# A seven-product second layer: sums in quarters, another product order, other places for loads and stores

## The chip, the cores and the metric

The kernel runs on one core of a Trainium2 chip. The time is the device time of one execution in microseconds (us); the kernel before takes 1622.39 us (median of 3 runs, 1622.34 to 1624.89). The profiled execution took 1622.71 us, of which 1620.9 us lie between its first and its last instruction (the span). Engines are named as in the profile: PE multiplies matrices, PEld loads its weights, DVE is the vector engine, ACT the scalar engine, POOL the GpSimd engine, SP issues the DMAs.

## The reference

```
q, k, v: (8, 8, 576, 64) f32
for each chunk of 64 tokens of each head:          # attention inside the chunk
    a = softmax(q_c @ k_c.T / sqrt(64)) @ v_c
x = a as (4608 tokens, 512)
x = silu(x @ w_in) @ w_out                         # 512 -> 2048 -> 512
h = x @ w_in2                                      # second network
out = (h * sigmoid(1.702 * h)) @ w_out2            # 4608 x 512
```

The weights come as f64 and are brought to f32 on the chip.

## The kernel before, in words

Every f32 operand is split in two fp32r tiles: a high part (a cast, on ACT) and the rest (operand minus high part, on DVE). A product is three matmuls: high by low, low by high, high by high.

**First stage, up to about 860 us.** Blocks of 512 tokens go through attention and the first network. PE works in steps of 24 matmuls (12 for `h`, 12 for the output). Beside it, every 7 steps, one piece of the second network's weights is prepared (`load_u`, `pack_w`, `combine_u` on POOL, `split_u`): 16 conversions in all. `split_u` runs twice per conversion, first for the four combinations that POOL made (`split_u(..., True)`), then for the three plain quarters. Each call takes one tile from the two-tile pool `r`, casts into it (ACT, L212), subtracts (DVE, L214) and stores it to HBM (L222). On the same DVE queue stand the two transposes `qkT` (L282) of each 128 tokens of attention; the scores on PE (L292) wait for them.

**Second network's first layer, to about 1211 us.** `in_products`, in seven products per 2 by 2 blocks (Strassen's scheme in Winograd's form) instead of eight.

**Second network's second layer, 1211 to 1575 us, where most of the change lies.** `out_products` takes 4 units of 1024 tokens. A unit has four quadrants A11, A12, A21, A22 of the activations (`g` in HBM, 256 KB per 128x512 block) and seven products with prepared weights: A11, A12, A22 and the sums S1 = A21 + A22, S2 = S1 - A11, S3 = A11 - A21, S4 = A12 - S2. Each product runs in 4 steps (`PAIRS`), so a unit has 28 steps, numbered from 0 in it. A step is 12 matmuls of 128x512 into two PSUM banks. The list `SEQ` gives the order of the products.

In a unit, per step: ACT casts an operand of 128x1024 (`high_d`, L938), DVE makes the low part (`low_d`, L943), both three steps ahead of PE. The tile for it comes from the pool `x` with 4 tiles, so the cast of step s+3 waits until PE has finished step s-1. POOL makes the 16 sums of a unit (`sum_d`, L925), 128x1024 each, in place: S1 and S2 and S4 over the tile `mix` (loaded with A21), S3 over the tile `a`. SP loads the other quadrants by `stream` into the pool `g` (3 tiles): a load waits until the third tile before it has been read. After a product's fourth step `finish_d` brings its two banks to SBUF: by two ACT copies (L981) or by two DVE additions to an earlier copy (L985). `turn_d` transposes on DVE (L1018), `store_d` stores (4 DMAs per 128x512).

Each engine works off its own queue in the order in which the program is written: the loop over steps calls, per step, stores, transposes, the entries of a table (`at_d(step, function, ...)`), `high_d` and `low_d` for three steps ahead, then the matmuls, then `finish_d`. The numbers in the table set the places; nothing is timed, an instruction waits only for its data and for the instruction before it.

**The last 512 tokens, 1575 us to the end.** `out_product`, with POOL sums of 128x256 (`sum_r`, L797) and DVE low parts (`split_r`, L810).

The lines that set this are few:

```python
SEQ = (A11, S1, S2, A12, S3, S4, A22)
BANK = {A11: "a", S2: "a", S3: "a", A22: "a", S1: "c", S4: "c", A12: "b"}
x_p = ctx.enter_context(tc.tile_pool(name="x", bufs=4))
g_p = ctx.enter_context(tc.tile_pool(name="g", bufs=LAG + 1))
nc.gpsimd.tensor_tensor(out=out_, in0=one, in1=two, op=op)      # L925
at(after, 0, s + 5, split_u, *key, True)
at(after, 0, s + 7, split_u, *key, False)
```

Of the kernel before, what the change touches and what calls it, by code (L numbers as in the profile page):

```python
# [17 lines left out]
P = 128  # L18
# [31 lines left out]
def chunk_attention_two_ffn(  # L50
# [823 lines left out]
    SEQ = (A11, S1, S2, A12, S3, S4, A22)  # L874
# [39 lines left out]
    def sum_d(u, o, pp):  # L914
# [32 lines left out]
    OPENS = {A11: "a", S1: "c", A12: "b"}  # L947
    BANK = {A11: "a", S2: "a", S3: "a", A22: "a", S1: "c", S4: "c", A12: "b"}

    def open_banks(u, name):  # L950

        if name == "a" and u % 2:
            whole = ps_at.tile([P, 2, N], F32, tag="at", name="ps_m")
            bank_u[u, name] = [whole[:, i] for i in range(2)]
        elif name == "b":
# [4 lines left out]
    def step_d(u, s):  # L960

        o, pp = SEQ[s // PAIRS], s % PAIRS
        if pp == 0 and o in OPENS:
            open_banks(u, OPENS[o])
# [27 lines left out]
    def finish_d(u, o):  # L992

        banks = bank_u[u, BANK[o]]
        if o == A11:
            kept_u["m1"] = [copy_d(st_p, "st", x) for x in banks]
        elif o == S1:
            kept_u["m5"] = [copy_d(v_p, "v", x) for x in banks]
        elif o == S2:
            kept_u["u2"] = [copy_d(*h, x) for h, x in zip(((v_p, "v"), (st_p, "st")), banks)]  # L1000
        elif o == A12:
            done_d.append((u, 0, 0, [add_d(x, y) for x, y in zip(banks, kept_u.pop("m1"))]))
        elif o == S3:
            done_d.append((u, 1, 1, [add_d(x, y) for x, y in zip(banks, kept_u.pop("m5"))]))
        elif o == S4:
            done_d.append((u, 0, 1, [add_d(x, y) for x, y in zip(banks, kept_u.pop("u2"))]))
        else:
            done_d.append((u, 1, 0, [copy_d(st_p, "st", x) for x in banks]))
# [3 lines left out]
    def turn_d():  # L1012

        while done_d:
            u, t, e, parts = done_d.pop(0)
            for i, s in enumerate(parts):
                to = st_p.tile([P, N], F32, tag="st", name="turned")
                nc.vector.transpose(out=to, in_=s)  # L1018
                turned_d.append(((2 * u + t) * N, (2 * e + i) * P, to))

    def store_d():

        while turned_d:
# [13 lines left out]
    def out_products():  # L1037
# [8 lines left out]
        at_d(1, sum_d, 0, S1, 3)  # L1046
# [421 lines left out]
```

## Time and profile before

| | us |
|---|---|
| median of 3 runs | 1622.39 |
| profiled execution | 1622.71 |
| its span | 1620.9 |
| PE busy (97% of the span) | 1564.9 |
| DVE busy (59%) | 959.8 |
| POOL busy (22%) | 352.1 |
| PE idle before matmuls of L970, ended by DVE | 33.3 |

Busy times are averages over stages with different limits. PE counts as busy while a matmul is in flight, so a step whose start was late can still look nearly full; how far apart the steps start says more.

### The profile page before, as it was taken

What the parts mean: (1) busy time and instruction counts of PE and PEld (TensorE: products, weight loads), DVE (VectorE), ACT (ScalarE), POOL (GpSimd) and SP (SyncE); (2) the same over time, 40 slices, a digit from 0 to 9 for tenths busy, and PEclk for the clock granted to TensorE, in tenths of its full rate; (3) what the DMA queues carried; (4) which work ended last, traced back from release to release, by engine and by line L of the source; (5) the groups of instructions that cost most, each with busy time, mean ns of one, the idle gap of its engine ahead of it and who ended that gap; (6) DMA issues with size and microseconds to landing.
All of it is one profiled execution on the core that took longest, in us unless ns stands there. A gap on an engine that the chain in (4) does not pass through costs nothing.

```text
span 1620.9 us, 24335 instructions
## 1 busy us (share of the span) xinstructions
PE 1564.9 (97%) x9226; PEld 1288.5 (79%) x9226; DVE 959.8 (59%) x1445; ACT 729.2 (45%) x1046; POOL 352.1 (22%) x211
## 2 busy tenths in 40 slices
PE   8999999999999999999999999999998999898998
PEld 6778888878887888788888888889876766676788
DVE  6986666666766676566223242424337697786875
ACT  6774444444444444444234454546443343333432
POOL 1000000000000000010110111113018275473935
PEclk9999999999999999999999999999999999999999
DMA  8763454444535444452555424334498554728363
GB/s 243 213 145 77 111 137 124 104 111 111 144 85 137 111 124 105 111 135 80 178 201 183 159 105 167 118 132 163 163 342 318 165 161 130 222 83 241 116 156 79
DMA packets 352951, 242.82 MB, mean 150 GB/s; under 512 B 261696, under 2 KB 284224, under 8 KB 348224
## 3 DMA queue, kind: packets, MB, share of 16 engines
q1 hardware_dynamic: 352832, 241.25, 50.2%
q8 instruction: 72, 1.18, 0.3%
q14 instruction: 47, 0.39, 0.1%
HBM read 155.19 MB, written 85.98 MB: 149 GB/s over the span
## 4 chain that ended last, share of the span: by engine, by line
PE 64%; DVE 10%; DMA 8%; POOL 7%; issue 4%; SPq 4%; ACT 3%; DVEq 0%; POOLq 0%; ACTq 0%
PE h L424 18%; PE acc L459 18%; PE acc L577 17%; DMA rows_s<-g 4%; DVE op L943 3%; POOL mix L925 3%; PE h L577 3%; POOL a L925 2%; PE ps_at L292 2%; PE ps_m L970 1%; SPq L1026 1%; DVE aT L383 1%; PE acc L829 1%; POOL raw_u L199 1%; SPq L257 1%
## 5 line engine op out<-in xcount | busy, mean ns | idle before, releaser
L424 PE MATMUL h<-x,w 128*128 128x512 f32 x1728 | 419.9, 392 | 0.6 <-DVE w L155 0.6
L459 PE MATMUL acc<-g,w 128*128 128x512 f32 x1728 | 416.5, 390 | 1.4 <-DVE w L155 1.2
L459 PEld LDWEIGHTS acc<-g,w 128*128 128x128 f32 x1728 | 323.6, 188 | 69.5 <-DVE w L155 1.9
L424 PEld LDWEIGHTS h<-x,w 128*128 128x128 f32 x1728 | 321.7, 188 | 69.7 <-DVE w L155 1.3
L577 PE MATMUL acc<-operand,t 128*128 128x512 f32 (+1 forms) x1200 | 274.4, 385 | 0.0
L577 PEld LDWEIGHTS acc<-operand,t 128*128 128x128 f32 x1200 | 222.4, 188 | 44.6
L447 DVE TENSOR_TENSOR g<-s,g 128x512 fp32r<-128x512 f32 x144 | 100.1, 697 | 217.5 <-ACT g L437 216.1
L435 ACT ACTIVATE s<-h 128x512 f32<-128x512 f32 x144 | 86.1, 598 | 301.3 <-PE h L424 295.2
L199 POOL TENSOR_TENSOR raw_u<-raw_u 128x256 f32<-128x256 f32 x64 | 52.6, 842 | 693.2 <-DVE raw_u L139 541.1
L970 PE MATMUL acc<-op,t 128*128 128x512 f32 x768 | 180.4, 394 | 8.7 <-DVE op L943 7.7
L970 PEld LDWEIGHTS acc<-op,t 128*128 128x128 f32 x768 | 144.3, 189 | 43.5 <-DVE op L943 12.2
L595 DVE TENSOR_TENSOR s<-acc,u 128x512 f32<-128x512 f32 (+1 forms) x80 | 51.0, 637 | 163.3 <-PE acc L577 120.2
L383 DVE STREAM_TRANSPOSE aT<-e 32x128 f32<-32x128 f32 x448 | 135.5, 303 | 6.0
L943 DVE TENSOR_TENSOR op<-mix,op 128x1024 fp32r<-128x1024 f32 x48 | 110.9, 2345 | 10.2 <-ACT op L938 9.8
L943 DVE TENSOR_TENSOR op<-rows_s,op 128x1024 fp32r<-128x1024 f32 x32 | 63.1, 1977 | 70.1 <-ACT op L938 69.7
L970 PE MATMUL ps_m<-op,t 128*128 128x512 f32 x384 | 94.1, 400 | 9.2 <-DVE op L943 9.2
L590 ACT COPY u<-acc 128x512 f32<-128x512 f32 (+1 forms) x80 | 43.5, 544 | 128.7 <-PE acc L577 128.4
L970 PEld LDWEIGHTS ps_m<-op,t 128*128 128x128 f32 x384 | 72.0, 191 | 30.7 <-DVE op L943 15.9
L925 POOL TENSOR_TENSOR mix<-mix,rows_s 128x1024 f32<-128x1024 f32 x16 | 50.5, 3176 | 201.9 <-DMA rows_s<-g 111.5
L437 ACT CAST g<-s 128x512 fp32r<-128x512 f32 x144 | 89.5, 622 | 4.6
L603 ACT ACTIVATE s<-s 128x512 f32<-128x512 f32 (+1 forms) x120 | 70.8, 591 | 33.8 <-DVE s L595 31.9
L938 ACT CAST op<-rows_s 128x1024 fp32r<-128x1024 f32 x32 | 33.6, 1049 | 116.1 <-DMA rows_s<-g 99.9
(128 smaller groups left out, 1739.7 us busy)
## 6 DMA issues: line engine op xcount, KB each, us to landing
g<-s SPq DMA_DIRECT2D x128, 256.0 KB, 2.1
rows_s<-g SPq DMA_DIRECT2D x128, 256.0 KB, 3.8
t<-w SPq DMA_DIRECT2D x28, 1024.0 KB, 5.4
w<-split_u SPq DMA_DIRECT2D x16, 1024.0 KB, 4.4
w<-split_u SPq DMA_DIRECT2D x16, 768.0 KB, 4.4
x<-o SPq DMA_DIRECT2D x36, 256.0 KB, 2.3
raw<-in_q_dram SPq DMA_DIRECT2D x256, 32.0 KB, 2.2
raw<-in_k_dram SPq DMA_DIRECT2D x256, 32.0 KB, 2.4
```

Source lines behind the costliest of these rows:

```text
L199: nc.gpsimd.tensor_tensor(out=high[:, t - T1], in0=one, in1=two, op=ALU.subtract)
L383: nc.vector.transpose(out=aT_t[t0][to:to + 32, j, u], in_=e[of:of + 32, c, r])
L424: nc.tensor.matmul(out=h[:, :n], lhsT=w[:, 0, a, c * P:(c + 1) * P], rhs=x[b][:, c, :n], start=(c == 0 and (a, b) == TERMS[0]), stop=(c == ...
L435: nc.scalar.activation(out=s[:, :n], in_=h[:, :n], func=ACTF.Silu)
L437: nc.scalar.copy(out=g[:, 0, :n], in_=s[:, :n])
L447: nc.vector.tensor_tensor(out=g[:, 1, :n], in0=s[:, :n], in1=g[:, 0, :n].bitcast(F32), op=ALU.subtract)
L459: nc.tensor.matmul(out=a[:, :n], lhsT=w[:, 1, wi, i * P:(i + 1) * P], rhs=g[:, gi, :n], start=first and (wi, gi) == TERMS[0], stop=last an ...
L577: nc.tensor.matmul(out=bank[:, :n], lhsT=of_t(0, j, WITH[o], a)[:, c * P:(c + 1) * P], rhs=x[:, b, c], start=start and (c, a, b) == terms[ ...
L603: nc.scalar.activation(out=s[:, :n], in_=src[:, :n], func=ACTF.Silu, scale=act_scale[1])
L925: nc.gpsimd.tensor_tensor(out=out_, in0=one, in1=two, op=op)
L943: nc.vector.tensor_tensor(out=t[:, 1], in0=source_d(u, o, pp), in1=t[:, 0].bitcast(F32), op=ALU.subtract)
L970: nc.tensor.matmul(out=bank, lhsT=of_t(1, 2 * pp + c, WITH[o], e)[:, i * P:(i + 1) * P], rhs=x[:, a, c], start=begins, stop=pp == PAIRS - ...
```

## The change

The numbers below are steps of a unit.

1. POOL's sums: one 128x1024 instruction becomes four of 128x256.
2. The products of a unit come as A11 S1 A22 S2 S3 A12 S4 instead of A11 S1 S2 A12 S3 S4 A22. A22 goes to the bank pair "b" and is copied from there (`m4`), and its output is S3's bank plus that copy, a second pair of DVE additions one step after the first (`late`). Bank pair "a" is now always the same two banks.
3. The places in the table: sums S1 at -3, -2, -1, 0, S2 at 2, 4, 5, 7, S3 at 9, 10, 12, 13, S4 at 15, 16, 18, 19 (before: -3 to 0, 2 to 5, 6 to 9, 10 to 13); loads of A22 for its own product at 1, 2, 3, 6 (before 19 to 22), A21 at 7, 8, 9, 11 (before 4 to 7), A12 at 12, 14, 15, 18 (before 8 to 11).
4. Per step one transpose and one store instead of all that are due; stores stand behind the table's entries; `finish_d` runs one step later, behind the `high_d` and `low_d` of that step.
5. First stage: `split_u(..., True)` at s + 6 instead of s + 5.

```diff
-    SEQ = (A11, S1, S2, A12, S3, S4, A22)
+    SEQ = (A11, S1, A22, S2, S3, A12, S4)
...
-            out_, one, two, op = mix, rows_s.pop((u, "a12", pp)), mix, ALU.subtract
-        nc.gpsimd.tensor_tensor(out=out_, in0=one, in1=two, op=op)
+            out_, one, two, op = mix, rows_s[u, "a12", pp], mix, ALU.subtract
+        for c in range(2):
+            for h in (slice(0, N // 2), slice(N // 2, N)):
+                nc.gpsimd.tensor_tensor(
+                    out=out_[:, c, h], in0=one[:, c, h], in1=two[:, c, h], op=op
+                )
...
-    OPENS = {A11: "a", S1: "c", A12: "b"}
-    BANK = {A11: "a", S2: "a", S3: "a", A22: "a", S1: "c", S4: "c", A12: "b"}
+    BANK = {A11: "a", S2: "a", S3: "a", A22: "b", A12: "b", S1: "c", S4: "c"}
+    OPENS = (A11, S1, A22, A12)
...
+        elif o == A22:
+            kept_u["m4"] = [copy_d(st_p, "st", x) for x in banks]
         elif o == S2:
             kept_u["u2"] = [copy_d(*h, x) for h, x in zip(((v_p, "v"), (st_p, "st")), banks)]
+        elif o == S3:
+            done(1, 1, "m5")
+            return lambda: done(1, 0, "m4")
...
-        while done_d:
-            u, t, e, parts = done_d.pop(0)
-            for i, s in enumerate(parts):
...
+        if done_d:
+            t0, d0, s = done_d.pop(0)
...
-                at_d(g + 4 + pp, stream, u, "a21", pp)
-                at_d(g + 8 + pp, stream, u, "a12", pp)
-                at_d(g + 19 + pp, lambda u, pp: stream(u, "a22o", pp), u, pp)
-                at_d(g + 2 + pp, sum_d, u, S2, pp)
-                at_d(g + 6 + pp, sum_d, u, S3, pp)
-                at_d(g + 10 + pp, sum_d, u, S4, pp)
...
+            at_each(u, "a22o", (1, 2, 3, 6))
+            at_each(u, "a21", (7, 8, 9, 11))
+            at_each(u, "a12", (12, 14, 15, 18))
...
+            sums_at(u, S2, (2, 4, 5, 7))
+            sums_at(u, S3, (9, 10, 12, 13))
+            sums_at(u, S4, (15, 16, 18, 19))
...
         for g in range(1, STEPS * NU):
             u, s = divmod(g, STEPS)
-            store_d()
-            turn_d()
             for fn, args in todo.get(g, ()):
                 fn(*args)
...
                 high_d(u3, o3, s3 % PAIRS)
                 low_d(u3, o3, s3 % PAIRS)
...
+            store_d()
+            if late is not None:
+                late()
+                late = None
+            if s % PAIRS == 0:
+                late = finish_d((g - 1) // STEPS, SEQ[(g - 1) % STEPS // PAIRS])
+            turn_d()
             step_d(u, s)
-            if s % PAIRS == PAIRS - 1:
-                finish_d(u, SEQ[s // PAIRS])
...
-            at(after, 0, s + 5, split_u, *key, True)
+            at(after, 0, s + 6, split_u, *key, True)
```

ACT's queue of the first unit around product S2, before (L938 casts an operand, L981 copies a bank). The casts from `mix` are the last two of S2's operands, those from `rows_s` A12's, that from `a11` the first of S3's; the copies from acc1 and acc3 empty S1's banks, those from acc0 and acc2 S2's:

```order
L938 CAST op_11326<-mix_11119 128x1024
L981 ACTIVATE o_11341<-acc1_11266 128x512
L981 ACTIVATE o_11343<-acc3_11267 128x512
L938 CAST op_11349<-mix_11119 128x1024
L938 CAST op_11370<-rows_s_11345 128x1024
L938 CAST op_11389<-rows_s_11366 128x1024
L938 CAST op_11408<-rows_s_11386 128x1024
L981 ACTIVATE o_11423<-acc0_11164 128x512
L981 ACTIVATE o_11425<-acc2_11165 128x512
L938 CAST op_11428<-rows_s_11405 128x1024
L938 CAST op_11446<-a11_10808 128x1024
```

The same queue in the changed kernel (the same two lines are L942 and L982 there), from S2's last cast over A22's copies out of `h` to the first casts of A12; acc0 and acc2 are again S2's banks:

```order
L942 CAST op_11458<-mix_11125 128x1024
L982 ACTIVATE o_11461<-h_11376 128x512
L982 ACTIVATE o_11463<-h_11377 128x512
L942 CAST op_11481<-a11_10808 128x1024
L942 CAST op_11499<-a11_10808 128x1024
L942 CAST op_11521<-a11_10879 128x1024
L942 CAST op_11540<-a11_10879 128x1024
L982 ACTIVATE o_11543<-acc0_11170 128x512
L982 ACTIVATE o_11545<-acc2_11171 128x512
L942 CAST op_11564<-rows_s_11451 128x1024
L942 CAST op_11591<-rows_s_11496 128x1024
```

S2's two copies now stand behind all four casts of the product that follows on PE (S3, from `a11`), the last of which is that of S3's fourth step; and S3 writes the same two banks.

POOL's queue, S2 and S3 of the last unit, before:

```order
L925 TENSOR_TENSOR mix_12212<-mix_12212,rows_s_12305 128x1024
L925 TENSOR_TENSOR mix_12163<-mix_12163,a11_12099 128x1024 x2
L925 TENSOR_TENSOR mix_12212<-mix_12212,a11_12134 128x1024 x2
L925 TENSOR_TENSOR a11_12099<-a11_12099,rows_s_12424 128x1024
L925 TENSOR_TENSOR a11_12099<-a11_12099,rows_s_12445 128x1024
```

and in the changed kernel:

```order
L927 TENSOR_TENSOR mix_12380<-mix_12380,rows_s_12410 128x256 x4
L927 TENSOR_TENSOR mix_12331<-mix_12331,a11_12191 128x256 x8
L927 TENSOR_TENSOR mix_12380<-mix_12380,a11_12214 128x256 x8
L927 TENSOR_TENSOR a11_12191<-a11_12191,rows_s_12610 128x256 x4
L927 TENSOR_TENSOR a11_12191<-a11_12191,rows_s_12632 128x256 x4
```

The sums follow each other as before; only their number of instructions has changed, four for one.

DVE's queue in the first stage, at two of the 16 conversions, as a difference. First the kind whose attention transposes (L282) came right behind the first low part (L214):

```order
 L447 TENSOR_TENSOR g_1891<-s_1889,g_1891 128x512
-L214 TENSOR_TENSOR split_u_1906<-raw_u_1644,split_u_1906 128x4x256
-L282 STREAM_TRANSPOSE qkT_1910<-raw0_1727 128x512
-L282 STREAM_TRANSPOSE qkT_1912<-raw1_1813 128x512
-L447 TENSOR_TENSOR g_1929<-s_1927,g_1929 128x512
+L282 STREAM_TRANSPOSE qkT_1906<-raw0_1727 128x512
+L282 STREAM_TRANSPOSE qkT_1908<-raw1_1813 128x512
+L447 TENSOR_TENSOR g_1925<-s_1923,g_1925 128x512
+L214 TENSOR_TENSOR split_u_1949<-raw_u_1644,split_u_1949 128x4x256
```

The transposes now stand ahead of the low part. Then the kind whose transposes come behind the second low part; they follow after the last row shown:

```order
-L214 TENSOR_TENSOR split_u_2710<-raw_u_2390,split_u_2710 128x4x256
-L383 STREAM_TRANSPOSE aT_2714<-e_2660 32x128 x16
-L447 TENSOR_TENSOR g_2746<-s_2744,g_2746 128x512
+L383 STREAM_TRANSPOSE aT_2710<-e_2660 32x128 x16
+L447 TENSOR_TENSOR g_2742<-s_2740,g_2742 128x512
+L214 TENSOR_TENSOR split_u_2757<-raw_u_2390,split_u_2757 128x4x256
 L447 TENSOR_TENSOR g_2776<-s_2774,g_2776 128x512
 L214 TENSOR_TENSOR split_u_2791<-raw_u_2390,split_u_2791 128x2x256
```

Here the first low part moved past sixteen small transposes, and only one instruction is left between it and the second low part, whose tile is free when the first part's store has landed.

## Rows read from the trace of the kernel before

**Rows 1.** PE in time order: start, length, operation, idle before and who ended it

```profile
1218.29 24.64 PE L970 MATMUL acc<-op,t 128*128 128x512 f32 x108
...
1254.43 4.36 PE L970 MATMUL h<-op,t 128*128 128x512 f32 x12 [4.94 <-DVE op L943]
...
1308.97 3.06 PE L970 MATMUL ps_m<-op,t 128*128 128x512 f32 x12 [0.33 <-DVE op L943]
...
1490.95 3.01 PE L970 MATMUL ps_m<-op,t 128*128 128x512 f32 x12 [0.33 <-DVE op L943]
...
1564.18 11.04 PE L970 MATMUL ps_m<-op,t 128*128 128x512 f32 x48
1575.06 1.59 PE L829 MATMUL acc<-t,half 128*128 128x256 f32 x12
```

**Rows 2.** Who ended PE's idle time before L970, 1200 to 1620 us

```profile
  DVE op L943: 33.3, 33
```

**Rows 3.** POOL's sums and DVE's low parts: minimum, median, maximum in ns

```profile
L925 POOL TENSOR_TENSOR mix<-mix,a x16: 3310/3378/3382, 1228.6 to 1512.1; 128x1024 f32<-128x1024 f32 x16
L943 DVE TENSOR_TENSOR op<-mix,op x48: 1181/3296/3420, 1221.8 to 1555.9; 128x1024 fp32r<-128x1024 f32 x48
```

**Rows 4.** The same for one sum, 1435 to 1437 us

```profile
L925 POOL TENSOR_TENSOR a<-a,rows_s x1: 2356/2356/2356, 1434.9 to 1434.9; 128x1024 f32<-128x1024 f32 x1
```

**Rows 5.** POOL and DVE in time order, last 512 tokens

```profile
1577.15 0.74 POOL L797 TENSOR_TENSOR sum_r<-sum_r,rows_r 128x256 f32<-128x256 f32 x1
1577.85 1.72 POOL L797 TENSOR_TENSOR sum_r<-rows_r 128x256 f32<-128x256 f32 x1
...
1577.48 1.49 DVE L810 TENSOR_TENSOR half<-sum_r,half 128x1024 fp32r<-128x1024 f32 x1 [1.71 <-ACT half L808]
```

**Rows 6.** The same sums grouped: busy us, mean ns, idle before

```profile
L797 POOL TENSOR_TENSOR sum_r<-rows_r 128x256 f32<-128x256 f32 x16 | 19.8, 1241 | 25.9 <-DMA rows_r<-g 25.9
```

**Rows 7.** PE and ACT in time order around the start of a step

```profile
1371.35 11.04 PE L970 MATMUL acc<-op,t 128*128 128x512 f32 x48
...
1371.59 1.06 ACT L938 CAST op<-mix 128x1024 fp32r<-128x1024 f32 x1 [1.67 <-PE ps_m L970]
...
1239.62 1.08 ACT L981 ACTIVATE o<-acc 128x512 f32<-128x512 f32 x2
```

**Rows 8.** POOL in time order, first unit

```profile
1222.51 6.11 POOL L925 TENSOR_TENSOR mix<-mix,rows_s 128x1024 f32<-128x1024 f32 x2 [7.54 <-DMA g<-s]
```

**Rows 9.** DMA issues: size, median us to landing; 1221:1233, then 1211:1575

```profile
rows_s<-g SPq DMA_DIRECT2D x6, 256.0 KB, 12.3
...
rows_s<-g SPq DMA_DIRECT2D x124, 256.0 KB, 3.7
```

**Rows 10.** PE's waits, 100:800: us in total, times, longest

```profile
PE ps_at L292 <- DVE qkT L282: 7.0, 4, 3.1
```

**Rows 11.** ACT and PE in time order at a conversion

```profile
651.03 1.11 ACT L212 CAST split_u<-raw_u 128x1024 fp32r<-128x1024 f32 x1 [6.59 <-POOL raw_u L199]
...
654.67 0.27 PE L292 MATMUL ps_at<-qkT 64*64 64x64 f32 x1 [3.10 <-DVE qkT L282]
```

**Rows 12.** DVE, PE, and the median landing of the store, another conversion

```profile
241.67 1.22 DVE L214 TENSOR_TENSOR split_u<-raw_u,split_u 128x1024 fp32r<-128x1024 f32 x1
242.81 5.04 DVE L383 STREAM_TRANSPOSE aT<-e 32x128 f32<-32x128 f32 x16
247.88 1.29 DVE L447 TENSOR_TENSOR g<-s,g 128x512 fp32r<-128x512 f32 x2
249.09 1.02 DVE L214 TENSOR_TENSOR split_u<-raw_u,split_u 128x512 fp32r<-128x512 f32 x2
250.03 1.30 DVE L282 STREAM_TRANSPOSE qkT<-raw 128x512 f32<-128x512 f32 x2
...
255.22 0.27 PE L292 MATMUL ps_at<-aT,v 64*64 64x64 f32 x1
...
w<-split_u SPq DMA_DIRECT2D x16, 1024.0 KB, 4.4
```

More of the change, by code (lines that the diff above doesn't have):

```diff
@@ L945, in low_d @@
         )
-    OPENS = {A11: "a", S1: "c", A12: "b"}
-    BANK = {A11: "a", S2: "a", S3: "a", A22: "a", S1: "c", S4: "c", A12: "b"}
+    BANK = {A11: "a", S2: "a", S3: "a", A22: "b", A12: "b", S1: "c", S4: "c"}
+    OPENS = (A11, S1, A22, A12)
     def open_banks(u, name):
[L952 to L955, printed above, removed]
+        if name == "b":
             bank_u[u, name] = [ps_h.tile([P, N], F32, tag="h", name="h") for _ in range(2)]
@@ L963, in step_d @@
         if pp == 0 and o in OPENS:
-            open_banks(u, OPENS[o])
+            open_banks(u, BANK[o])
         x = op_t.pop((u, o, pp))
@@ L994, in finish_d, with done @@
         banks = bank_u[u, BANK[o]]
+        def done(t, e, kept):
+            done_d.extend(
+                ((2 * u + t) * N, (2 * e + i) * P, add_d(x, y))
+                for i, (x, y) in enumerate(zip(banks, kept_u.pop(kept)))
+            )
         if o == A11:
-            kept_u["m1"] = [copy_d(st_p, "st", x) for x in banks]
+            kept_u["m1"] = [copy_d(v_p, "v", x) for x in banks]
         elif o == S1:
-            kept_u["m5"] = [copy_d(v_p, "v", x) for x in banks]
+            kept_u["m5"] = [copy_d(st_p, "st", x) for x in banks]
+        elif o == A22:
+            kept_u["m4"] = [copy_d(st_p, "st", x) for x in banks]
         elif o == S2:
             kept_u["u2"] = [copy_d(*h, x) for h, x in zip(((v_p, "v"), (st_p, "st")), banks)]
+        elif o == S3:
+            done(1, 1, "m5")
+            return lambda: done(1, 0, "m4")
         elif o == A12:
[L1002 to L1006, printed above, removed]
-        else:
-            done_d.append((u, 1, 0, [copy_d(st_p, "st", x) for x in banks]))
+            done(0, 0, "m1")
+        else:
+            done(0, 1, "u2")
+        return None
     turned_d = []
     def turn_d():
-        while done_d:
-            u, t, e, parts = done_d.pop(0)
-            for i, s in enumerate(parts):
-                to = st_p.tile([P, N], F32, tag="st", name="turned")
-                nc.vector.transpose(out=to, in_=s)
-                turned_d.append(((2 * u + t) * N, (2 * e + i) * P, to))
+        if done_d:
+            t0, d0, s = done_d.pop(0)
+            to = st_p.tile([P, N], F32, tag="st", name="turned")
+            nc.vector.transpose(out=to, in_=s)
+            turned_d.append((t0, d0, to))
     def store_d():
-        while turned_d:
+        if turned_d:
             t0, d0, s = turned_d.pop(0)
@@ L1082, in out_products @@
                     rows_s.pop((u3, "a22o", s3 % PAIRS))
+            store_d()
+            if late is not None:
+                late()
+                late = None
+            if s % PAIRS == 0:
+                late = finish_d((g - 1) // STEPS, SEQ[(g - 1) % STEPS // PAIRS])
+            turn_d()
             step_d(u, s)
-            if s % PAIRS == PAIRS - 1:
-                finish_d(u, SEQ[s // PAIRS])
+        finish_d(NU - 1, SEQ[-1])
         for q in range(NR):
```

24 lines of the change are left out of this document (14 added, 10 removed).

## The prediction

> **What bounds the kernel now.** I read first PE in order of time, because PE is busy nearly throughout and only the distance between the starts of its steps shows what is lost. In the second layer a step that waits for nothing takes 2.72 us: the last four before the tail start at 1564.18 and are over at 1575.06 [rows 1]. From step 1 of the first unit (1218.29) to the tail there are 111 steps, 301.9 us at that rate, and they take 356.8: 54.9 us are lost [rows 1]. By unit: 90.7 us for 27 steps in the first (17.2 lost), 182.0 for the next 56 (29.7 lost), 84.1 for the last 28 (7.9 lost).
>
> Second, who ended PE's idle time there: DVE's low part, every time [rows 2]. The rest of the 54.9 us is restarts and slow steps behind gaps: the step behind a gap of 4.94 us took 4.36 us where others behind a short gap take 3.06 [rows 1], 1.3 us more.
>
> Third, why DVE is late. Its low part takes 1.18 us at best, 3.30 in the median beside `mix`; POOL's sum of 128x1024 takes 3.38 us in the median, 2.36 when DVE is idle [rows 3, 4]. 2.36 plus one low part is about 3.4: while POOL sums, the two take turns by whole instructions, and DVE makes an operand every 3.3 to 3.4 us where PE uses one every 2.72. Sixteen sums at 3.38 are 54 us of a unit's 76.2, packed into the 17 steps from -3 to 13; and A22's own rows come last, when the loads of the next unit stand in the same queue.
>
> Fourth, the first stage. PE waits four times, 7.0 us in all, for attention's transposes on DVE [rows 10]; at such a place ACT's first cast of a conversion waited 6.59 us for POOL, DVE's low part waited for it, and the transposes stood behind [rows 11].
>
> **The change, part by part.**
>
> Sums in quarters. In the tail POOL already makes sums of 128x256. Two in a row start 0.70 us apart, one with a low part of 128x1024 in between takes 1.72 instead of 0.74, and that low part 1.49 instead of 1.18 [rows 3, 5]. So a sum is 4 x 0.70 = 2.80 us and each low part in its time adds 0.98; with a low part per 2.72 us it lasts T = 2.80 + 0.98 T/2.72, T = 4.38 us. DVE's part is then 1.5 us against 2.72: DVE is no longer late of itself. POOL works 16 x 4.38 = 70 us of a unit's 76.2, so that order decides whether it is in time. Bounds for T: a quarter of the whole sum, 0.59 a piece [rows 4], gives 2.36/0.64 = 3.7; the mean piece of the tail, 1.24 [rows 6], gives 5.0. I take 4.38, the one worked out at this mix.
>
> The Trainium skill speaks against this edit less than the rows do: its GPSIMD Engine Reference, section "Elementwise — side-by-side cycle accounting", charges `tensor_tensor` by the element (4497 ns for 2048), so four quarters would cost what the whole does, an estimate of 0.56 us each. The rows have 0.74 for a quarter alone and 2.36 for the whole, some 0.6 us dearer in four. What the page's price would make of the time is the second rival.
>
> Order and places. In steps of a unit: the first half of `mix` is loaded once S4's second low part is done (about step 23), landing in the median 3.7 us [rows 9] after some 0.5 us of issue, so S1's first sum starts near 24.5 of the unit before, -3.5. Twelve sums later, 12 x 4.38 = 52.5 us = 19.3 steps, S3's last sum is ready at 15.8. S2 is needed from step 9 on and ready from 4.6, S4 from 21 and ready from 17.4; all loads have a step or more to spare. SP's stores now stand behind the table's loads and hold none of them up. So nothing waits for POOL in a settled unit, but for S3's last sum the margin is 0.3 of a step.
>
> The wait that the change adds: S3 follows S2 in the same two banks, and S2's two copies stand on ACT behind the cast of S3's fourth step, which needs the tile of S2's last step. That cast starts 0.24 us after the step is over (1371.59 against 1371.35), takes 1.05, the first copy 0.54 [rows 7]: PE waits 1.8 us, 1.9 with its restart, in each unit. If S3's last sum is late, PE waits for it here too, three steps earlier than for its operand. For the thin margin I add 1.0 per unit: 2.9 in each of units 2 to 4, 8.7.
>
> First unit. S1's third sum can start when its rows land, at 1222.51 [rows 8]; that hangs on the loads before and stays. Ten sums from there end at 1222.5 + 43.8 = 1266.3, some 1.9 earlier because DVE stops with PE, 1264.4. Step 15 is over at 1218.29 + 15 x 2.72 = 1259.1. Cast and copy make it 1266.0: a wait of 6.9, and 1.3 for the slow step behind it, as above. A22's last rows are asked for near 1235 and land 3.7 to 12.3 us later [rows 9]; midway, 1243.2, is 0.3 us late. First unit 8.5. With T = 3.7 it is 2.2, with T = 5.0 15.
>
> Sum of this stage: 54.9 lost before, 8.5 + 8.7 = 17.2 after: 37.7 gained. Bounds: with T = 3.7, 2.2 + 3 x 1.9 = 7.9 lost, 47.0 gained; with T = 5.0, S3's last sum is ready at 18.6, 6.7 us late, 8.3 per unit with cast and copy, 15 + 24.9 = 39.9 lost, 15.0 gained.
>
> Transposes and additions spread over steps, two more additions for two copies fewer: DVE has 28 x 1.5 + 16 x 0.65 = 52 us of 76; I cost them at nothing. If a transpose stands ahead of a low part it costs 0.7 us of a lead of two steps. The tail keeps its work.
>
> First stage. With the first cast one step later the transposes no longer stand behind it at the four places: 7.0 us gone. But both tiles of a conversion go through one slot, and the second cast, a step behind now, waits for the first one's store. At the kind of conversion in [rows 12]: the sixteen transposes from 241.7 to 246.7, one subtraction of 0.65, the low part until 248.6, the store landed 4.4 later at 253.0, two casts and the second low parts until 254.7, the attention transposes until 256.0, where PE wants them at 255.2: 0.8 us each, four times, 3.2. At the other kinds ACT waits up to 4.5 us, with two steps of 5.4 us before its result is used. Net 3.8 gained; bounds 7.0 gained (store in time) and nothing gained (store 1 us slower).
>
> Total: 37.7 + 3.8 = 41.5 off the profiled execution's 1622.71 gives 1581.2; the median lies 0.3 below that execution, so 1580.9.
>
> **The rivals.**
>
> POOL becomes the bound (T = 5.0). For it: POOL's margin is 0.3 of a step, and a piece is 1.24 us in the tail's mean [rows 6]. Against: there two low parts come per four pieces, here 1.6. 1622.4 - 15.0 - 3.8 = 1603.6.
>
> Cheaper pieces, T = 3.7: POOL is ahead everywhere, the first unit waits 2.2 us. For it: the whole sum alone, 2.36 [rows 4]. Against: 0.70 between pieces [rows 5]. 1622.4 - 47.0 - 3.8 = 1571.6. This is where the Trainium skill's price by the element, above, leads.
>
> The quarters don't do what they are for: DVE's low part still waits for four pieces. Then 16 low parts at 3.38 lose 10.6 us a unit, less two steps of lead, 5.2, plus the copies' wait 1.9: 7.1 a unit, 13.7 in the first, 35.0 lost, 19.9 gained: 1598.7. Against it the 1.49 of [rows 5].
>
> Slower than before: POOL's sixteen sums take longer than a unit took. A unit took 356.8/111 x 28 = 90.0 us; with the first stage's 3.8 us the point is 90.9/64 = 1.42 us per piece. At 1.47 (twice 0.735) a unit takes 94.1, and four make 1622.4 + 16.4 - 3.8 = 1635. It would need that DVE's additions and transposes hold POOL up as low parts do, which gives 64 x 0.70 + 28 x 0.98 + 16 x 0.65 = 82.6, 1.29 a piece, and still more.
>
> **How the numbers follow.** Forecast 0.57 (within 10 us of 1580.9), cheaper pieces 0.17, POOL the bound 0.14, quarters without effect 0.06, slower 0.04, and 0.02 that gains and waits cancel. About 0.2% (3.2 us) can be told from no change: faster 0.94, same 0.02, slower 0.04. The range runs from the cheap pieces with the whole 7.0 us of the first stage (1568), a little below, 1565, to POOL as the bound with nothing of it, 1607.
>
> **What would show it.** Right: sums of about 4.4 us in four pieces, low parts at 1.2 to 1.7, steps 2.72 apart over long stretches, one wait per unit before S3's first step, ended by ACT's copy, near 2 us and about 7 in the first unit; in the first stage, PE's waits for the transposes fewer and near 0.8. Wrong: PE waiting for low parts in the middle of S3 or S4, low parts of 2 us and more, a wait before S3 that grows from unit to unit, or ACT's second cast of a conversion holding up PE.

## The result, and the profile after

The changed kernel takes 1579.45 us (median of 6 runs, 1578.12 to 1582.65), the kernel before 1623.02 (6 runs): a ratio of 0.9732, with a 95% interval of 0.9720 to 0.9745. The forecast was 1580.9. The profiled execution took 1578.65 us, its span is 1576.9, 44.0 shorter than before.

PE in time order in the changed kernel's second layer, columns as in [rows 1]; the rows with an idle time are the first steps of S3 in the four units:

```profile
1212.17 19.20 PE L971 MATMUL acc<-op,t 128*128 128x512 f32 x84
...
1259.21 13.87 PE L971 MATMUL acc<-op,t 128*128 128x512 f32 x48 [6.08 <-ACT o L982]
...
1340.29 11.19 PE L971 MATMUL acc<-op,t 128*128 128x512 f32 x48 [1.93 <-ACT o L982]
...
1418.43 11.19 PE L971 MATMUL acc<-op,t 128*128 128x512 f32 x48 [1.68 <-ACT o L982]
...
1496.96 12.77 PE L971 MATMUL acc<-op,t 128*128 128x512 f32 x48 [2.06 <-ACT o L982]
...
1531.34 1.59 PE L829 MATMUL acc<-t,half 128*128 128x256 f32 x12
```

From step 1 to the tail it is 319.2 us where 301.9 are needed: 17.25 lost instead of 54.85 [rows 1], so 37.6 us of the 44.0 come from here. 6.1 lie ahead of it (step 1 starts at 1212.17 instead of 1218.29), 0.3 in the tail. All 33 waits for low parts [rows 2] are gone; one wait per unit is left, ended by ACT's copy.

POOL's sums, then DVE's low parts, grouped as in [rows 3]; then POOL in time order, second unit, S1 to S3:

```profile
L927 POOL TENSOR_TENSOR mix<-mix,a x64: 731/742/1787, 1223.4 to 1476.5; 128x256 f32<-128x256 f32 x64
...
L947 DVE TENSOR_TENSOR op<-mix,op x48: 1175/1336/1804, 1214.7 to 1521.8; 128x1024 fp32r<-128x1024 f32 x48
```

```profile
1285.65 17.84 POOL L927 TENSOR_TENSOR mix<-mix,rows_s 128x256 f32<-128x256 f32 x16 [11.80 <-DMA mix<-g]
1303.45 17.16 POOL L927 TENSOR_TENSOR mix<-mix,a 128x256 f32<-128x256 f32 x16
1320.58 18.08 POOL L927 TENSOR_TENSOR a<-a,rows_s 128x256 f32<-128x256 f32 x16
```

Twelve sums take 53.0 us, 4.42 each; low parts take 1.34 in the median instead of 3.30.

What ACT's casts waited for is followed in the rest of this document. The first row is that of the kernel before (1211 to 1575 us), the second that of the changed one (1200 to 1577): us in total, times, longest.

```profile
ACT op L938 <- DMA rows_s<-g: 99.9, 25, 9.0
```

```profile
ACT op L942 <- DMA rows_s<-g: 7.9, 5, 2.8
```

The first of these rows was there to be read before the prediction, and its working doesn't use it. It is time that ACT waited, not time that PE lost; how much of it reached PE the experiments have to show.

### The profile page after: what moved, and what is told of

Its sections match the earlier page's. It is cut to its first block, busy times and chain, and to the rows that moved or that the text cites. A ratio compares the mean times of both kernels' runs of the same rounds, so it can differ in the third digit from the quotient of the medians.

```text
span 1576.9 us, 24560 instructions
## 1 busy us (share of the span) xinstructions
PE 1548.5 (98%) x9226; PEld 1286.8 (82%) x9226; DVE 882.0 (56%) x1453; ACT 731.0 (46%) x1046; POOL 416.3 (26%) x403
## 4 chain that ended last, share of the span: by engine, by line
PE 81%; DVE 6%; DMA 5%; POOL 3%; issue 2%; ACT 2%; SPq 1%; DVEq 0%; ACTq 0%; POOLq 0%
PE acc L459 20%; PE h L424 20%; PE acc L577 18%; PE acc L971 10%; PE h L971 3%; PE h L577 3%; POOL a L927 2%; DMA rows_s<-g 2%; PE ps_at L292 2%; PE acc L829 1%; DVE aT L383 1%; DMA w<-split_u 1%; DVE g L447 1%; PE h L829 1%; DMA raw_w<-in_moe_w_in_dram 1%
## 5 line engine op out<-in xcount | busy, mean ns | idle before, releaser
L971 PE MATMUL acc<-op,t 128*128 128x512 f32 x960 | 224.7, 395 | 11.7 <-ACT o L982 11.7
L971 PEld LDWEIGHTS acc<-op,t 128*128 128x128 f32 x960 | 183.0, 191 | 51.9 <-ACT o L982 13.4
L927 POOL TENSOR_TENSOR mix<-mix,rows_s 128x256 f32<-128x256 f32 x64 | 69.3, 1118 | 115.9 <-DMA rows_s<-g 84.2
L971 PE MATMUL h<-op,t 128*128 128x512 f32 x384 | 88.3, 389 | 0.0
L947 DVE TENSOR_TENSOR op<-mix,op 128x1024 fp32r<-128x1024 f32 x48 | 67.1, 1403 | 35.5 <-ACT op L942 35.0
L971 PEld LDWEIGHTS h<-op,t 128*128 128x128 f32 x384 | 72.1, 188 | 14.9
L942 ACT CAST op<-mix 128x1024 fp32r<-128x1024 f32 x48 | 50.3, 1053 | 72.2 <-PE h L971 36.8
L947 DVE TENSOR_TENSOR op<-rows_s,op 128x1024 fp32r<-128x1024 f32 x32 | 46.7, 1458 | 55.1 <-ACT op L942 48.4
```

The lines of the kernel that those rows point to most:

```text
L927: nc.gpsimd.tensor_tensor(out=out_[:, c, h], in0=one[:, c, h], in1=two[:, c, h], op=op)
L947: nc.vector.tensor_tensor(out=t[:, 1], in0=source_d(u, o, pp), in1=t[:, 0].bitcast(F32), op=ALU.subtract)
L971: nc.tensor.matmul(out=bank, lhsT=of_t(1, 2 * pp + c, WITH[o], e)[:, i * P:(i + 1) * P], rhs=x[:, a, c], start=begins, stop=pp == PAIRS - ...
```

## The experiments

"Lost" is counted as in [rows 1]: from step 1 to the tail in PE's order of time, less 111 x 2.72 us, and by unit in the same way. Each run stood beside runs of the kernel before on its chip.

| kernel | us | ratio to before (95%) | lost: units 1, 2, 3, 4 |
|---|---|---|---|
| before | 1623.0 | | 54.9: 17.2, 16.4, 13.3, 7.9 |
| changed | 1579.5 | 0.9732 (0.9720 to 0.9745) | 17.3: 9.1, 2.2, 2.0, 4.0 |
| whole_sums | 1573.4 | 0.9693 (0.9674 to 0.9711) | 8.5: 2.5, 2.0, 2.0, 2.0 |
| before_quarters | 1638.4 | 1.0092 (1.0071 to 1.0113) | 63.2: 16.1, 17.9, 18.0, 11.2 |
| cast_early | 1586.7 | 0.9770 (0.9751 to 0.9788) | 20.4: 11.9, 2.3, 2.0, 4.2 |
| copies_first | 1571.6 | 0.9675 (0.9658 to 0.9693) | 9.8: 6.1, 1.3, 1.1, 1.3 |
| mix_later | 1616.3 | 0.9952 (0.9937 to 0.9967) | 47.1: 13.3, 11.9, 12.0, 10.0 |
| no_a21_rows | 1620.1 | 0.9976 (0.9964 to 0.9988) | 52.4: 15.8, 15.4, 13.2, 8.0 |
| both_late_rows | 1612.4 | 0.9935 (0.9918 to 0.9953) | 45.2: 10.4, 11.8, 10.2, 12.8 |
| no_rows_through_pool | 1602.5 | 0.9868 (0.9848 to 0.9887) | 32.6: 8.2, 11.1, 8.8, 4.5 |
| stores_ahead | 1573.2 | 0.9689 (0.9675 to 0.9703) | 9.6: 2.8, 2.0, 2.7, 2.0 |
| whole_copies_swap | 1567.8 | 0.9660 (0.9643 to 0.9676) | 6.8: 4.2, 1.1, 1.2, 0.3 |
| quarters_copies_swap | 1567.0 | 0.9649 (0.9636 to 0.9661) | 6.9: 3.1, 1.3, 1.3, 1.3 |
| halves_copies_swap | 1564.3 | 0.9632 (0.9620 to 0.9644) | 3.0: 2.0, 0.3, 0.3, 0.3 |

### The quarters alone, both ways round

whole_sums, in the changed kernel:

```diff
-        for c in range(2):
-            for h in (slice(0, N // 2), slice(N // 2, N)):
-                nc.gpsimd.tensor_tensor(
-                    out=out_[:, c, h], in0=one[:, c, h], in1=two[:, c, h], op=op
-                )
+        nc.gpsimd.tensor_tensor(out=out_, in0=one, in1=two, op=op)
```

> The changed kernel with POOL's sums as one 128x1024 again, all else as changed. Theory (a low part can only start between two POOL instructions, so the length of the piece decides): low parts beside the sums back near 3.3 us in the median, a sum 3.4 us, PE stopped by DVE's low part again, 35 us lost in the second layer instead of 17.2: 1597 us (1590 to 1610). Rival (the order of the products and the places of loads and stores carry the gain, the size of the pieces little): 1575 to 1585, PE not stopped by low parts.

before_quarters is the reverse of this edit, in the kernel before.

> The kernel before with quarter sums alone: old order of products, old places, old first stage. Theory (the quarters carry the gain): low parts 1.3 to 1.5 us, hardly a wait for them on PE; no wait before S3, since A12 lies between S2 and S3; a sum takes 4.4 us in a table made for 3.4, so S4's last sum comes about half a step late, 1 to 2 us per unit, and the first unit loses 5 to 8: 12 lost instead of 54.9, 1580 us (1572 to 1592). Rival (without the new order and places POOL at 4.4 us a sum is late for S3 and S4 by several us in each unit): 1600 us or more.

Measured: 1573.4 and 1638.4. The theory of the prediction fell both ways: without the quarters the change gains more, and the quarters without the rest make the kernel slower. The low parts do what was said. In whole_sums those from `a` take 3.26 us in the median, and yet PE waits for the copies alone, but for 0.2 us once in the first unit; its low parts, then the one row on the layer among PE's longest waits:

```profile
L943 DVE TENSOR_TENSOR op<-a,op x32: 1175/3260/3432, 1204.3 to 1494.2; 128x1024 fp32r<-128x1024 f32 x32
```

```profile
PE acc L967 <- ACT o L978: 6.7, 4, 1.7
```

Why slow low parts cost nothing here is seen in its second unit, DVE first, then PE, in time order:

```profile
1286.46 7.28 DVE L943 TENSOR_TENSOR op<-a,op 128x1024 fp32r<-128x1024 f32 x3
...
1316.59 13.45 DVE L943 TENSOR_TENSOR op<-mix,op 128x1024 fp32r<-128x1024 f32 x4
1329.97 11.20 DVE L943 TENSOR_TENSOR op<-a,op 128x1024 fp32r<-128x1024 f32 x4
```

```profile
1279.46 32.80 PE L967 MATMUL acc<-op,t 128*128 128x512 f32 x144
...
1322.98 11.04 PE L967 MATMUL acc<-op,t 128*128 128x512 f32 x48
```

The first row of DVE ends at 1293.74 with the operand of step 3; PE starts that step at 1279.46 + 7 x 2.72 = 1298.50, 4.8 us later (steps 0 to 3 are the fifth to eighth in PE's first row). The second ends at 1330.04 with that of step 15, PE starts it at 1322.98 + 3 x 2.72 = 1331.14, 1.1 us later. DVE falls back by some 0.6 us (3.36 - 2.72) with each low part beside a sum, but it came in with a lead, and each low part that meets no sum (1.2 us) gives 1.5 back. The lead can be some 5.6 us: the three steps that the cast stands ahead, 8.16, less 0.24 for its start, 1.05 for the cast [rows 7] and 1.2 for the low part. In the kernel before, the third unit is entered with little lead. Steps 26 and 27 of its second unit, first DVE, then ACT, then PE:

```profile
1390.94 1.22 DVE L943 TENSOR_TENSOR op<-rows_s,op 128x1024 fp32r<-128x1024 f32 x1 [4.17 <-ACT op L938]
...
1395.79 1.23 DVE L943 TENSOR_TENSOR op<-rows_s,op 128x1024 fp32r<-128x1024 f32 x1 [1.21 <-ACT op L938]
```

```profile
1394.71 1.05 ACT L938 CAST op<-rows_s 128x1024 fp32r<-128x1024 f32 x1 [3.80 <-DMA rows_s<-g]
```

```profile
1392.22 3.02 PE L970 MATMUL ps_m<-op,t 128*128 128x512 f32 x12 [2.38 <-DVE op L943]
1397.07 4.61 PE L970 MATMUL ps_m<-op,t 128*128 128x512 f32 x12 [1.82 <-DVE op L943]
```

These low parts take 1.2 us, POOL makes no sum, and PE still waits: the cast before the second waited for A22's rows. In before_quarters ACT's casts wait longer for rows, and for POOL's sums 71.3 us where the kernel before has 20.9 (last row). That is what the rival said: sums of 4.4 us in a table made for 3.4. What ACT's casts and then PE waited for:

```profile
ACT op L942 <- DMA rows_s<-g: 111.4, 30, 9.5
ACT op L942 <- POOL mix L927: 71.3, 30, 4.0
```

```profile
PE h L974 <- DVE op L947: 28.3, 5, 7.5
```

```profile
ACT op L938 <- POOL mix L925: 20.9, 10, 3.9
```

In the new order the price of the quarters, some 6 us, lies for the most part ahead of S3, where the copies stand behind a cast that waits for POOL: the first unit loses 9.1 instead of 2.5. Where that wait is shorter (the last three kernels) quarters cost nothing that can be measured, 1567.0 us against 1567.8 with whole sums.

### Why the rows are late in the old order

mix_later, in the kernel before (the change moves the loads of `mix` in this way too, to 23 and 25, although the list of its parts doesn't name it):

```diff
-                    at_d(g + 20 + 2 * h, load_a21, u + 1, h)
+                    at_d(g + 23 + 2 * h, load_a21, u + 1, h)
```

> The kernel before with one edit: the next unit's loads into mix stand at steps 23 and 25 instead of 20 and 22, so behind A22's own rows in SP's queue. New theory (before lost its time because rows land late: ACT's casts waited 99.9 us for them, and A22's rows stood behind loads that wait for the tile of mix): no waits for A22's rows in steps 24 to 27 of units 1 to 3, 6.7 us and some 1.3 behind them each, 24 us gained: 1600 us (1592 to 1608); ACT's waits for rows at half. Rival (the alternation of low part and sum sets the pace): as before, 1618 to 1626.

no_a21_rows, in the kernel before:

```diff
-            out_, one, two, op = a11, a11, rows_s.pop((u, "a21", pp)), ALU.subtract
+            out_, one, two, op = a11, a11, mix, ALU.subtract
...
-                at_d(g + 4 + pp, stream, u, "a21", pp)
```

> The kernel before without the loads of A21's rows for S3 (left out: S3 is formed as A11 minus mix, so the output is another); the sums, their lengths and their order stay. New theory (A12's rows land late because their slots are held by A21's rows until POOL has made S3's sums): the waits before A12's first step go, 9 us in the first unit and 2.6 in each of the others, while A22's stay: 1606 us (1598 to 1613). Rival (the alternation sets the pace, or A12's rows are late for another reason): 1618 to 1626.

both_late_rows holds both edits.

> The kernel before with both edits of the runs before: mix loaded later, and A21's rows not loaded (left out: S3 is A11 minus mix, so the output is another). Sums, their lengths and the order of products stay. Theory (rows that land late at two places of a unit, each of which hides the other; only with both gone does DVE keep a lead over PE): much more than the 7.8 and 4.0 us of the two alone: some 26 us lost in the layer instead of 54.9, 1595 us (1588 to 1602). Rival (the two add up, and the rest is the alternation of low part and sum): 1612 us (1608 to 1616).

no_rows_through_pool adds one to that:

```diff
-            out_, one, two, op = mix, rows_s.pop((u, "a12", pp)), mix, ALU.subtract
+            rows_s.pop((u, "a12", pp))
+            out_, one, two, op = mix, mix, mix, ALU.subtract
```

> The run with both late rows, and beside that S4's sums no longer read A12's rows (left out: S4 is mix minus mix, so the output is another): all sixteen sums of 3.4 us stay where they are, but the tiles of A12's rows come free when DVE has read them, not when POOL has. Theory (in the old order the rows that PE needs at steps 12 to 15 wait for tiles that POOL's ninth to thirteenth sum hands back): the wait at step 15, 4.9 us with 2 to 2.8 of slow matmuls behind it in each unit, goes: 3 to 5 lost per unit instead of 10 to 13, 1583 us (1578 to 1590). Rival (the alternation of low part and sum, or the start of the next unit's sums, sets the unit's time): 1603 to 1613.

The last three leave loads or an operand out, so that their output is another.

Measured: 7.8, 4.0 and 12.0 us gained by the first three, where 24, 18 and 29 were expected. The two edits add up, and both together take what the rival said, 1612 us. Each time the wait moved rather than went: with mix later, A12's first step waits 4.9 us instead of 2.6; without A21's rows it is A12's fourth step. Lost by steps of a unit, the four units together, worked out as in the table above (the first unit from step 1 on):

| kernel | steps 0 to 6 | 7 to 19 | 20 to 27 |
|---|---|---|---|
| before | 4.9 | 31.4 | 18.6 |
| mix_later | 0.0 | 42.3 | 4.8 |
| no_a21_rows | 4.8 | 32.1 | 15.5 |
| both_late_rows | 0.0 | 44.7 | 0.5 |
| no_rows_through_pool | 0.0 | 17.9 | 14.6 |

So later loads of `mix` cure most of what is lost at A22's steps and behind them, 18.7 us, and cost 11.0 at the steps between. They make POOL's sums late: ACT's casts in mix_later wait for them 49.9 us instead of 20.9.

```profile
ACT op L938 <- POOL mix L925: 49.9, 24, 5.0
```

PE and ACT in both_late_rows, second unit, in time order:

```profile
1344.72 3.06 PE L970 MATMUL h<-op,t 128*128 128x512 f32 x12 [0.28 <-DVE op L943]
1352.67 5.49 PE L970 MATMUL h<-op,t 128*128 128x512 f32 x12 [4.90 <-DVE op L943]
```

```profile
1350.29 1.05 ACT L938 CAST op<-rows_s 128x1024 fp32r<-128x1024 f32 x1 [11.42 <-DMA rows_s<-g]
```

A12's four tiles of rows share three slots and are held until POOL has made S4's sums, so the fourth is loaded after POOL's thirteenth sum. Where no sum holds a row back (no_rows_through_pool) this wait is gone and the lost time falls by another 12.6 us, to 32.6. That rows held until POOL is done delay PE is thereby shown, but it is worth a third of what was expected (10 us against 29), and the time, 1602.5, is the rival's, not the theory's. One thing beside the rows is another in this run: S4's sums, with an operand left out, take 2.87 us.

What is left is of two kinds. PE in the second unit:

```profile
1327.56 3.03 PE L971 MATMUL ps_m<-op,t 128*128 128x512 f32 x12 [0.32 <-DVE op L944]
1330.90 3.03 PE L971 MATMUL ps_m<-op,t 128*128 128x512 f32 x12 [0.31 <-DVE op L944]
...
1375.68 14.07 PE L971 MATMUL ps_m<-op,t 128*128 128x512 f32 x48 [2.63 <-DVE op L944]
```

Steps 8 to 13 lie 3.3 us apart, as the prediction had it; the whole stretch from step 7 (1321.34) to step 20 (1362.00) loses 5.3. The last unit loses 4.5 us, all of it in this stretch; PE's steps 10 and 11, DVE's steps 6 to 11, and what ACT waited for longest from 1486 to 1534 us:

```profile
1502.27 3.06 PE L971 MATMUL ps_m<-op,t 128*128 128x512 f32 x12 [0.33 <-DVE op L944]
1505.62 3.02 PE L971 MATMUL ps_m<-op,t 128*128 128x512 f32 x12 [0.29 <-DVE op L944]
```

```profile
1486.54 19.02 DVE L944 TENSOR_TENSOR op<-mix,op 128x1024 fp32r<-128x1024 f32 x6 [3.68 <-ACT op L939]
```

```profile
ACT op L939 <- POOL mix L926: 12.7, 6, 4.2
```

No cast waits for rows here, and DVE was ahead: step 5's low part is done at 1482.87, 5.3 us before PE starts that step. The cast for step 6 waits for a sum, which leaves 2.0 us, and the six low parts beside sums take the rest: the last ends at 1505.56, as step 11 starts. The kernel before loses its lead in the same way in its first unit, ahead of its first wait for rows (DVE's steps 4 to 11, PE's step 11, the first cast that waits for rows):

```profile
1221.80 24.57 DVE L943 TENSOR_TENSOR op<-mix,op 128x1024 fp32r<-128x1024 f32 x8 [1.69 <-ACT op L938]
```

```profile
1246.43 3.06 PE L970 MATMUL acc<-op,t 128*128 128x512 f32 x12 [0.31 <-DVE op L943]
```

```profile
1252.07 1.04 ACT L938 CAST op<-rows_s 128x1024 fp32r<-128x1024 f32 x1 [9.02 <-DMA rows_s<-g]
```

So the alternation does stop PE, with rows in time, where sums follow one another without a pause: each low part beside one takes 0.6 us of a lead of some 5.6. In this run that stretch keeps 17.9 us of the 32.6. How much of it comes from the alternation and how much from sums that start late, behind the later loads of `mix`, wasn't tried apart.

The other 14.6 lie at A22's steps: its rows are late again. They share the DMA queue with the next unit's loads; the kernel before from 1368 to 1400 us, the queue (packets, MB, share of 16 engines) and the issues:

```profile
q1 hardware_dynamic: 14071, 8.60, 91.3%
...
rows_s<-g SPq DMA_DIRECT2D x15, 256.0 KB, 5.0
```

5.0 us to landing, against 3.7 over the layer [rows 9]. The queue is not the only candidate: SP issues loads and stores in one order, and in the kernel before it stood 86.6 us for transposes, with loads behind the stores that needed them; in the changed kernel 12.9 (second row, to 1535 us).

```profile
SPq L1026 <- DVE turned L1018: 86.6, 12, 16.8
```

```profile
SPq L1035 <- DVE turned L1027: 12.9, 8, 8.8
```

No run moves the stores in the old order, so whether they made rows late there is open. So is what the new order and what the new places took away of the 24 us between this kernel (32.6 lost) and whole_sums (8.5).

### The stores, and the first stage

stores_ahead, in whole_sums (all that are due, at the head of the step and no longer behind the table's entries):

```diff
+            store_d()
+            turn_d()
             for fn, args in todo.get(g, ()):
...
-        if done_d:
+        while done_d:
...
-        if turned_d:
+        while turned_d:
```

> The changed kernel with whole sums (1573.4 us) and, beside that, stores and transposes as in the kernel before: all that are due at once, ahead of the step's loads and casts. Theory (places of loads and order of products carry the gain; stores wait for transposes on SP and hold loads up only where these are due): two transposes in a row cost a low part 0.7 us of its lead and stores delay loads by 1 to 3 us, which a lead of 1 us at the end of S2 does not always cover: 1573 to 1580, 1576 the value. Rival (stores in front of loads were what made rows late): 1590 or more.

Measured 1573.2 against 1573.4: in the new order, with whole sums, the new places of stores and transposes are worth nothing that can be measured. SP's wait for transposes didn't come back with the old places, so this run doesn't try what the old order had (1211 to 1525 us):

```profile
SPq L1031 <- DVE turned L1023: 10.6, 4, 8.2
```

cast_early, in the changed kernel:

```diff
-            at(after, 0, s + 6, split_u, *key, True)
+            at(after, 0, s + 5, split_u, *key, True)
```

> The changed kernel with the first layer's first cast of a conversion one step earlier, as before. Theory (the one-step move took away PE's waits for attention's transposes and put smaller ones in their place): PE waits four times for the transposes, 7.0 us in all, instead of 2.5 us: 4.5 us longer, 1584 us; by the working of the prediction 3.8. Rival (the waits are hidden or the clock gives them back): within 0.2% of the changed kernel, 1576 to 1582.

Measured 1586.7: 7.2 us more by the medians, 6.2 by the ratios (0.9770 against 0.9732). PE's waits for the transposes between 100 and 800 us, first in the changed kernel, then in cast_early:

```profile
PE ps_at L292 <- DVE qkT L282: 2.5, 3, 1.7
```

```profile
PE ps_at L292 <- DVE qkT L282: 6.2, 5, 1.9
```

That is 3.7 of it, and step 1 starts 5.2 us later. Behind the longest of these waits the granted clock is 0.60 from 327 to 330 us, where the changed kernel has 1.00; the rest of the other 1.5 isn't shown. The layer itself lost 20.4 instead of 17.3 in this execution; the reason is open.

### The wait before S3, and the fastest version

copies_first, in the changed kernel:

```diff
+            if s == 4 * PAIRS:
+                finish_d(u, S2)
             if u3 < NU:
...
-            if s % PAIRS == 0:
+            if s % PAIRS == 0 and s != 4 * PAIRS:
                 late = finish_d((g - 1) // STEPS, SEQ[(g - 1) % STEPS // PAIRS])
```

> The changed kernel with S2's two copies placed ahead of the cast of S3's fourth step on ACT, instead of behind its cast and low part. Theory (the four waits before S3, 11.7 us, and the slow matmuls behind two of them, 4.9 us, come from the copies standing behind that cast): each wait shrinks to 0.2 to 0.7 us, no slow matmuls, 15 us gained: 1564.5 us (1562 to 1568). Rival (POOL's last sum of S3 is late anyway, so that PE waits for it three steps later instead): the first unit still loses 3 to 6 us and the later ones 1 each: 1572 us.

Measured 1571.6, as the rival said. In the first unit, though, 2.3 of the 6.1 us lost are a wait for the low part of A22's first step, which neither theory had; only 1.6 are the wait before S3. The copies now stand behind the cast of S3's third step, and that one waits for POOL's third sum, ACT in the second unit in time order:

```profile
1335.96 1.05 ACT L942 CAST op<-a 128x1024 fp32r<-128x1024 f32 x1 [2.72 <-POOL a L927]
1336.91 1.08 ACT L982 ACTIVATE o<-acc 128x512 f32<-128x512 f32 x2
```

So the sums at 4.4 us are late for S3 by one cast more. The last three kernels put this edit together with an exchange in the first layer,

```diff
-            at(after, 0, s + 6, split_u, *key, True)
-            at(after, 0, s + 7, split_u, *key, False)
+            at(after, 0, s + 5, split_u, *key, False)
+            at(after, 0, s + 7, split_u, *key, True)
```

(and the raw tile is given back by the later call), with the sum whole, in quarters, and in halves:

```diff
+        for c in range(2):
+            nc.gpsimd.tensor_tensor(out=out_[:, c], in0=one[:, c], in1=two[:, c], op=op)
```

> The changed kernel with whole sums, S2's copies ahead of the cast of S3's fourth step, and in the first layer's conversions the three plain quarters at s + 5 and the four combinations at s + 7 instead of the other way round (the plain ones don't wait for POOL, and two steps lie between the two that share a slot). Theory: the four waits before S3 fall from 1.68 to some 0.6 us with whole sums, 4.3 gained; PE's waits for attention's transposes fall from 2.5 to 3.6 us to under 1, 2.5 gained: 1566.5 us (1564 to 1570). Rival (two low parts of a conversion further apart meet the transposes again): first stage as in the kernel before, 1571 to 1573.

> The same with the quarters of the changed kernel. Theory: low parts 1.2 to 1.8 us, but a sum of 4.4 us makes S3's third and fourth sums late, so that the copies of S2, behind the third cast, start 1 us late in each unit, as in the run with copies first: 1569 us (1566.5 to 1571.5), slower than whole sums by 1 to 2 us. Rival (shorter low parts are worth more than timely sums): 1563 to 1566.

> The fastest kernel so far (1567.75 us, whole sums, copies first, conversions swapped) with sums as two of 128x512. Theory: a low part waits for at most one half (some 1.25 us by a whole sum of 2.36), so it takes at most 2.5 us, under the 2.72 of a step, and DVE's lead isn't used up; a sum lasts some 3.9 us, in time for S3. The six short waits for low parts (1.8 us) and the shorter slow steps around them go: 1565.5 us (1563 to 1568). Rival (any longer sum makes S3 late, as quarters did): 1569 to 1572.

Measured 1567.8, 1567.0 and 1564.3, all within the ranges that were expected, but quarters were to be slower than whole sums by 1 to 2 us and are not. Halves are the fastest kernel of the study; against quarters on the same chip the two intervals still touch. Its sums and low parts:

```profile
L926 POOL TENSOR_TENSOR mix<-mix,a x32: 1280/2271/2291, 1225.7 to 1465.9; 128x512 f32<-128x512 f32 x32
...
L944 DVE TENSOR_TENSOR op<-mix,op x48: 1177/1484/2344, 1217.1 to 1509.9; 128x1024 fp32r<-128x1024 f32 x48
```

No low part exceeds 2.4 us, less than a step, so DVE needs no lead; the layer loses 3.0 us, 1.7 of them in one wait for a copy in the first unit.

## Why the prediction was right in its time and wrong in its main reason

**"Third, why DVE is late"** is the step that failed: it makes the alternation the whole cause of the 54.9 us. The alternation is real, 3.4 us per low part and sum, one after the other, in every kernel with whole sums. But it stops PE only when DVE's lead is used up: whole_sums has the same low parts and loses 8.5 us. In the old order the lead goes in two ways: to sums that follow one another without a pause, where casts wait for sums too, and to casts that wait for rows (99.9 us). The first is the prediction's own; its size was not worked out, and it keeps 17.9 us where the rows are in time. The second it names ("A22's own rows come last, when the loads of the next unit stand in the same queue") and puts at nothing, without a reason. It followed the chain from PE to DVE and stopped before ACT's cast and the rows. Three edits on the rows gain 22.3 of the 54.9 in the layer, and another 14.6 lie where rows still are late; how the two ways divide in the kernel before stays open. A hint stood in its first part: the last unit loses only 7.9 us, the others 13 to 17, and the last has no next unit whose loads its A22 rows meet.

**"Sums in quarters", as the source of the gain:** wrong in sign. In the old order they cost 15 us by the ratios (8.3 in the layer's profile), in the new one about 6 (8.8 in the layer's profile). Their own numbers held: 4.42 us a sum against 4.38 forecast, low parts 1.34 against 1.5.

**"Order and places", costed as a wait and nothing else:** this part carries the gain, 46.4 us in the layer (54.9 lost before, 8.5 in whole_sums). How it does so is argued from the traces, not shown by a run: A22's rows are read by ACT and DVE alone; put at steps 8 to 11 they give POOL eight more steps before A12's rows are wanted, the loads of the next unit no longer meet rows that PE needs at once, and the sums lie over 23 steps instead of 17. The order of products and the places of the loads weren't taken apart. The places of the stores have no share in the new order (stores_ahead); in the old one they weren't tried.

**Why the sum came out:** 17.2 lost were forecast after, and 17.25 measured, because the sum for the changed kernel worked with its own POOL time and its own queues; the 54.9 before were a count, whatever their cause. The terms: the first unit 8.5 against 9.1 (wait 6.9 against 6.1, slow matmuls 1.3 against 2.8); units 2 to 4 8.7 against 8.2, where the waits were 1.7 to 2.1 for 1.9 forecast, and the added 1.0 for the thin margin was needed only in the last, for slow matmuls (1.7) and not for POOL. That the sum comes so close, 17.2 to 17.25, is luck in part: errors of 0.8 and 1.5 us in the first unit cancel. S3's last sum was ready at step 16.2 of the second unit ((1338.66 - 1294.68) / 2.72) against 15.8, so the wait was in part POOL's: 1.93 us where whole_sums has 1.68.

**First stage:** 3.8 forecast, 4.5 by the waits (7.0 [rows 10] to 2.5), 5.2 in cast_early up to step 1, with what stands behind the waits. The new wait is where it was put: the second cast of a conversion waits for the store, then the transposes and PE, here in ACT's and DVE's order of time:

```profile
252.73 0.97 ACT L212 CAST split_u<-raw_u 128x512 fp32r<-128x512 f32 x2 [5.86 <-DMA w<-split_u]
```

```profile
254.35 1.30 DVE L282 STREAM_TRANSPOSE qkT<-raw 128x512 f32<-128x512 f32 x2
```

PE waits 1.7 us here, 0.4 at the two other places, against 0.8 four times. Another 1.0 us of the 6.1 ahead of step 1 is a wait of the layer's first step for the last work of the first layer, which the profile of before has and that of the changed kernel has not (whole_sums has it at 0.8 again).

**The rivals.** "The quarters don't do what they are for" had the outcome right and the price of it wrong: 1598.7 was to be the price of whole sums in the new order, which take 1573.4. (In its sum two steps of lead are put at 5.2 us; they are 5.4, and its 7.1 a unit goes by that.) What it describes is seen in the old order instead: 10.6 less 5.4 makes 5.2 us a unit, and in no_rows_through_pool the last two units lose 4.0 and 4.5 in steps 7 to 19. The time came out 8 us above "cheaper pieces" (3.7 us a sum; the second unit has 4.42). The Trainium skill's price by the element (GPSIMD Engine Reference, "Elementwise — side-by-side cycle accounting"), which stood behind that rival, would have four quarters cost what the whole does. The same section of the Trainium skill names a dispatch per instruction for this engine too, without a figure; the rows have 0.15 to 0.2 us more for each piece (last section).

## What to carry to other kernels

Follow a wait until its releaser is no longer waiting itself, and ask of an engine that alternates with another with what lead it enters that stretch and how long the stretch is: a slow rate costs nothing until the lead is spent (here 0.6 us a step from some 5.6), and a pause gives it back. Before cutting an instruction up, undo it in thought in the new order as well as the old: in the last three kernels it was enough that a piece and its neighbour fit in one step (1.3 + 1.2 us in 2.7), and shorter pieces gained nothing. A forecast that meets its number is no evidence for its reasons: here the quarters, which were to gain 37.7 us in the layer together with their order, cost 8.8, and the order, which was priced as a wait, gained 46.4.

## What the runs showed of the hardware

A wait of 2 us can cost nearly its own length again in clock, and not each time. Windows of the changed kernel (us, busy times, then the granted clock): behind the wait of 6.08 us, behind that of 1.93, behind that of 2.06:

```profile
1262.00:1264.70 2.70, 2.70 (x8) 2.11 (x7) 0.00 (x0) 0.00 (x0) 2.70 (x4) 0.50 0.59 209
...
1340.29:1343.00 2.71, 2.71 (x12) 2.24 (x13) 0.82 (x1) 0.43 (x1) 2.71 (x3) 1.00 0.92 321
1497.00:1499.70 2.70, 2.70 (x7) 2.12 (x8) 0.79 (x1) 0.40 (x1) 2.70 (x3) 0.52 0.48 166
```

0.50 is the lower of the clock's two levels, 1.2 GHz of 2.4. In the first and the last window the granted clock is near it, in the middle one it is full. The first wait costs 2.8 us more and the last 1.7 (their rows of four steps above, 13.87 and 12.77, against 11.04); the middle one costs 0.15. The sum in pieces: 128x256, 128x512 and 128x1024 take 0.73, 1.28 and 2.36 us where no low part falls between, so each piece has a fixed cost of about 0.2 us by these lengths; quarters in a row start 0.70 us apart [rows 5], which makes it 0.15.
